# ssm_k by channels and turned on TensorE in an AdaLN / long-convolution / token-mixer kernel

## The chip, the cores and the metric

The kernel runs on one core of a Trainium2 chip. The metric is the device time of one execution in microseconds (us). Everything is float32; the large products of the mixer run as split float32 products, outside the part that is changed.

## The reference

Only what the changed part computes is kept. S is 2048 tokens, D 640 channels.

```python
mod = (silu(c) @ w_mod)                       # six rows of 640: sa, ca, ga, sb, cb, gb
h  = layernorm(q) * (1 + ca) + sa
k_shift = causal depthwise conv of k with shift_k (4 taps per channel)
kv = k_shift * v
y  = irfft(rfft(kv padded to 2S) * rfft(ssm_k padded to 2S))[:S] + kv * ssm_D
x  = q + ga * (h * y)
# then: layernorm of x, modulation with cb and sb, the token mixer (w1, gelu, w2), times gb, plus x
```

`kv * ssm_D` is done by adding `ssm_D` to element 0 of each channel's filter `ssm_k`.

## The kernel before

**Stages.** The 640 channels go in NC = 5 groups of DC = 128, `c` = 0 to 4. The long convolution of a group is a transform written as matrix products. *Step one* (`step1(side, t)`, line 222) multiplies by the constant F1, in four tiles `t` for each side: side 0 is kv, side 1 the filter; a tile is 16 matmuls into one PSUM buffer, which ScalarE copies into Z (line 232). *f2* (`f2(g)`, line 236), eight tiles a group, is the second step of both sides at once: 32 matmuls (line 246), a ScalarE copy (line 250), two VectorE products (`mul`) and two POOL combinations (`add`) into Y. *i2* and *i1* (lines 267 and 285) go back: i2 writes T2, which is the second half of the tile T_z; i1 needs the constant V1, and its PSUM result is gated: VectorE multiplies it into A1 (`gate`, line 311), POOL adds A1 to the rows of q. A1 is prepared as (q normalised) times G1 plus G0: ScalarE writes the 16 normalised row tiles (`ac`, line 301), VectorE multiplies and adds (`po`). After the last group the mixer follows, some 390 us that the change does not touch.

**Orders.** The schedule is written out by hand: each engine runs its instructions in the order of the text. In the loop over `c`, the f2 of group `c` is followed by step one of side 0 of the next group, i2, i1 with the gates, and step one of side 1 of the next group; then f2 of the next group. Three PSUM buffers go round (`psum()`, `ring`); a fourth, `tap`, holds the taps and sums of kv and also the products of w_mod. Loads go out on SP's queue, at the start some on ScalarE's.

**The first group.** kv of a group is made in four parts `g` (`kv_ops`): part 2 on POOL, 0, 1 and 3 on VectorE, eight operations of 128x512 each, into the tile X (`T_x` are other tiles, for the rows of q). The taps lie in TR, a part of the tile T_rows; `load_taps` loads them and `all_taps` copies them. At the start the parts of kv of group 0 are made while SP loads group 1 (`kv_loads`), then step one of side 0 runs on TensorE, then kv of group 1, then step one of side 1.

**The filter.** `load_ks` (line 162) brings ssm_k of a group by time, in pieces of 32 numbers, two loads of 512 KB into KSR (the first half of T_aux), and ssm_D as a row; `perm_add` (line 170) adds ssm_D, on POOL or VectorE; `perm` (line 175) is one ScalarE copy of 128x2048 into KSP (the tile P), the operand of step one's side 1. P also holds f2's products later. The ssm_k of group 1 can be loaded only after w_mod's pieces 2 and 3 have been read, since they lie in T_aux.

**The modulation.** `load_q` (line 512) loads the 32 half tiles of q and pieces 0 to 3 of w_mod; piece 4 follows after f2. `mod_part` (line 350) is a product of one piece (line 354, six matmuls), `mod_sum` a ScalarE copy of the sum, `mod_row(i)` (line 361) spreads a row over the partitions into G0, G1. VectorE's statistics of q (lines 561, 562) follow f2 of group 0, then `rstd` (line 334) takes the root on ScalarE and Newton steps on VectorE. In the tail of group 0 the order is: step one of side 0, a transposition (line 572) of the biases and of `c` with silu, i2(0), products 0 to 3, rstd, four rows of `ac`, i2(1), product 4, mod_sum, `ac`, kv part 2 on POOL, mod rows, taps, `perm_add(1)`, `perm(1)`, `ac`, `po`, i1 with the gates, step one of side 1.

## Time and profile before

| | |
|---|---|
| runs | 703.35 us median of 3 (703.0 to 708.99) |
| profiled execution | 706.67 us, its span 704.6 us |
| mean granted TensorE clock in it | 0.976 |
| busy | PE 641.4, PEld 620.4, DVE 501.5, ACT 307.8, POOL 156.1 us |
| DMA | 89.36 MB, mean 127 GB/s over the span |
| first step one starts / first f2 starts | 23.22 / 40.87 us |
| f2 of group 1 starts | 110.63 us |

PE is TensorE's matmuls, PEld its weight loads, DVE VectorE, ACT ScalarE, POOL GpSimd, SP the engine that issues most DMAs. Times within the execution count from the start of its span. The profile names a group of instructions by line, engine, operation and tile (out<-in); line 60 is the helper that records every VectorE and POOL tensor operation, so such rows are told apart by their tiles. A matmul of the program stands twice in the profile's counts where both operands are plain float32.

### The profile page before, as it was taken

The page shows a single profiled execution, that of the slowest core. Times are in us where ns is not written, and L with a number is a line of the kernel's source. Part 1 is how long each engine was busy: PE and PEld are TensorE (multiplying, and loading weights), DVE is VectorE, ACT ScalarE, POOL GpSimd, SP SyncE. Part 2 cuts the span into 40 slices and gives each one's busy share as a digit, 9 for nine tenths or more (in the row PEclk, how much of TensorE's full clock was granted, in tenths as well). Part 3 has the DMA queues.
Part 4 walks back from the last instruction along what each step waited for, and adds up shares of the span by engine and source line. Part 5 has one row for each costly group of instructions (what it writes and reads, how often), then busy time and mean ns, then how long its engine had stood idle before and what let it go on. Part 6 is the DMA issues. An engine that isn't in the chain of part 4 may idle for free.

```text
span 704.6 us, 20705 instructions
## 1 busy us (share of the span) xinstructions
PE 641.4 (91%) x9078; PEld 620.4 (88%) x9078; DVE 501.5 (71%) x846; ACT 307.8 (44%) x463; POOL 156.1 (22%) x135
## 2 busy tenths in 40 slices
PE   0699769999999999978888999999999999999997
PEld 0699569989989989758878999999999999999997
DVE  7688578969878638679886430564377699888886
ACT  0664644635745545345766420431243332333331
POOL 5297058625527328100010000000000000000000
PEclk9999979999999899799999999999999999999999
DMA  9978978346433522334030833357385634555511
GB/s 182 213 217 263 325 159 176 86 78 143 78 68 92 151 56 70 114 83 98 1 60 22 158 62 59 78 130 160 112 234 152 205 116 128 153 170 171 155 52 39
DMA packets 170848, 89.36 MB, mean 127 GB/s; under 512 B 89571, under 2 KB 160518, under 8 KB 170758
## 3 DMA queue, kind: packets, MB, share of 16 engines
q1 hardware_dynamic: 166210, 86.73, 48.8%
q10 hardware_dynamic: 4548, 1.31, 1.1%
q8 instruction: 71, 1.16, 0.7%
q14 instruction: 19, 0.16, 0.1%
HBM read 74.25 MB, written 13.76 MB: 125 GB/s over the span
## 4 chain that ended last, share of the span: by engine, by line
PE 67%; DVE 14%; DMA 6%; POOL 5%; ACT 4%; issue 3%; SPq 0%; ACTq 0%; DVEq 0%; POOLq 0%
PE pst L1059 20%; PE pst L446 17%; PE pst L246 8%; PE pst L230 7%; PE pst L275 6%; POOL y L60 4%; PE pst L1123 4%; PE pst L947 3%; DMA aux<-in_A_ssm_k_dram 3%; PE pst L294 2%; DVE aux L60 2%; DVE tap L60 1%; DVE p L60 1%; PE tap L354 1%; DVE kt L60 1%
## 5 line engine op out<-in xcount | busy, mean ns | idle before, releaser
L246 PEld LDWEIGHTS pst<-z,w 128*64 128x64 f32 x2560 | 94.7, 141 | 7.7 <-ACT z L232 7.3
L246 PE MATMUL pst<-z,w 128*64 128x64 f32 x2560 | 95.7, 240 | 6.2 <-ACT z L232 6.1
L60 POOL TENSOR_TENSOR y<-p 128x256 f32<-128x256 f32 x72 | 92.5, 1353 | 24.3 <-DVE p L60 23.9
L60 DVE TENSOR_TENSOR p<-pst,kt 128x512 f32<-128x512 f32 x80 | 52.6, 693 | 22.1 <-ACT kt L250 15.9
L230 PE MATMUL pst<-v,x 128*64 128x128 f32 x640 | 45.8, 304 | 23.2 <-POOL t L471 23.2
L232 ACT ACTIVATE z<-pst 128x1024 f32<-128x1024 f32 x40 | 45.8, 1144 | 43.9 <-PE pst L230 25.9
L230 PEld LDWEIGHTS pst<-v,x 128*64 128x64 f32 x640 | 43.8, 221 | 23.7 <-issue 23.2
L1059 PE MATMUL pst<-r_z,m_w 128*128 128x320 f32 x259 | 48.5, 309 | 1.3 <-DVE m_w L60 1.3
L275 PEld LDWEIGHTS pst<-v,y 32*128 32x128 f32 x1280 | 43.3, 210 | 6.5 <-POOL y L60 2.7
L275 PE MATMUL pst<-v,y 32*128 32x64 f32 x1280 | 45.3, 297 | 2.8 <-DVE y L60 2.1
L1047 ACT ACTIVATE m_w<-m_v 128x896 fp32r<-128x896 f32 x30 | 27.8, 948 | 42.6 <-DVE m_v L60 27.4
L230 PE MATMUL pst<-v,p 128*64 128x128 f32 x640 | 40.0, 284 | 7.0 <-DVE aux L60 4.9
L250 ACT ACTIVATE kt<-pst 128x512 f32<-128x512 f32 x40 | 25.2, 631 | 48.0 <-PE pst L246 25.6
L230 PEld LDWEIGHTS pst<-v,p 128*64 128x64 f32 x640 | 37.4, 143 | 8.3 <-DVE aux L60 5.1
L1059 PEld LDWEIGHTS pst<-r_z,m_w 128*128 128x128 f32 x259 | 40.6, 188 | 1.5 <-DVE m_w L60 1.5
L60 DVE TENSOR_TENSOR m_w<-m_v,m_w 128x896 fp32r<-128x896 f32 x30 | 32.5, 1087 | 11.2 <-ACT m_w L1047 11.2
L853 ACT ACTIVATE pst<-pst,sm 128x640 f32<-128x640 f32 x14 | 10.7, 767 | 59.3 <-PE pst L446 59.3
L60 DVE TENSOR_TENSOR tap<-tap,kt 128x512 f32<-128x512 f32 x51 | 35.6, 698 | 1.3
L60 DVE TENSOR_TENSOR kt<-in,tap 128x512 f32<-128x512 f32 x51 | 35.1, 688 | 1.5
L1059 PE MATMUL pst<-h_x,m_w 128*128 128x320 f32 x168 | 33.7, 309 | 0.0
L283 ACT ACTIVATE z<-pst 128x512 f32<-128x512 f32 x38 | 21.4, 665 | 27.9 <-PE pst L275 27.9
L1047 ACT ACTIVATE m_w<-m_p 128x896 fp32r<-128x896 f32 x13 | 12.4, 954 | 44.5 <-DVE m_p L60 27.6
(310 smaller groups left out, 1395.6 us busy)
## 6 DMA issues: line engine op xcount, KB each, us to landing
x<-in_B_w_dram SPq DMA_DIRECT2D x20, 512.0 KB
m_v<-in_B_w_dram SPq DMA_DIRECT2D x19, 384.0 KB
aux<-in_A_ssm_k_dram SPq DMA_DIRECT2D x10, 512.0 KB
m_x<-xs SPq DMA_DIRECT2D x32, 160.0 KB
out_dram<-m_x SPq DMA_DIRECT2D x32, 160.0 KB
in<-in_A_k_dram SPq DMA_DIRECT2D x36, 128.0 KB
in<-in_A_v_dram SPq DMA_DIRECT2D x36, 128.0 KB
x<-in_B_w_dram SPq DMA_DIRECT2D x10, 384.0 KB
```

Source lines behind the costliest of these rows:

```text
L60: TT = lambda eng, o, a, b, op: eng.tensor_tensor(o, a, b, op=op)
L230: pe.matmul(ps[64 * ri:64 * ri + 64, o:o + 128], lhs, F1[:, 128 * ri:128 * ri + 128], start=True, stop=True)
L232: evac = lambda: act.activation(Z[:, side, t].rearrange("p a k e -> p e a k"), ps.rearrange("p (e a k) -> p e a k", a=8, e=2), AF.Copy)
L246: pe.matmul(ps[64 * h:64 * h + 64, o:o + 64], W2[k1 // 32][:, 2 * (k1 % 32) + ri], rhs, start=True, stop=True)
L250: act.activation(kt.rearrange("p (m i) -> p m i", i=32), pv[:, :, 1], AF.Copy)
L275: pe.matmul(pp[qd // 2][:, o:o + 64], Y[p, ri, i:i + 2].rearrange("p i k -> p (i k)"), V2[p, 64 * ri:64 * ri + 64], start=ri == 0, stop=ri ...
L283: act.activation(o, i, AF.Copy)
L446: pe.matmul(ps[0:m, h, 0:320], w_.bitcast(F32R), r_[:, 320 * h:320 * h + 320].bitcast(F32R), start=first and i == 0, stop=last and i == 2)
L947: pe.matmul(ps[n][:, h, 0:320], sets[n][:, j].bitcast(F32R), r[:, 320 * h:320 * h + 320].bitcast(F32R), start=j == 0 and r is hh, stop=j = ...
L1047: act.activation(W[n][0].bitcast(F32R), A[p, w_], AF.Copy)
L1059: pe.matmul(bank[n], w[:, i].bitcast(F32R), r.bitcast(F32R), start=i == 0 and k == 0, stop=i == 6 and k == 2)
L1123: pe.matmul(acc[s][:, h, 0:320], w[:, f_].bitcast(F32R), u[r + h].bitcast(F32R), start=f_ == 0 and k == 0, stop=f_ == NF - 1 and k == 2)
```

## The change

- ssm_k of groups 0 and 1 is loaded by channels (`load_kc`, one load of 1 MB, 8 KB a channel) into KSR, and `turn` brings it into KSP: 64 small matmuls against an identity (EYE, loaded into a part of T_rows) into two PSUM buffers, and four ScalarE copies. ssm_D is loaded as columns (`dcol`) and added by one ScalarE (group 0) or POOL (group 1) instruction of 128x1. Groups 2 to 4 keep `load_ks`, `perm_add` and `perm`.
- The first ssm_k is issued behind the first part of v, ahead of the rest of v; the order of v stays 0, 2, 1, 3. The first w2 constant goes out behind the first v load of group 1.
- kv of group 0 goes into T_y (`x0`), and X is left to group 1; kv of group 1 is now written ahead of step one in the text.
- Step one of group 0: tiles 0 and 1 of side 1, then the four of side 0, then tiles 2 and 3 of side 1.
- q and w_mod: q 0 to 3, piece 0, q 4 to 7, piece 1 and the taps before f2; q 8 to 15, piece 3 and ssm_k of group 1 in f2's fourth tile; pieces 2 and 4, now in the second half of T_z, after f2. The transposition and silu move into f2's sixth tile.
- In the tail of group 0: the five products right after step one (order 0, 1, 3, 2, 4), the loads of k and v of group 2, mod_sum, i2(0), mod rows 0 and 1, rstd, mod row 2, eight rows of `ac`, i2(1), eight rows, all of `po`, then kv part 2 on POOL, `turn`, the taps, the next `load_ks`.

The order on each engine follows the text of both kernels.

```diff
@@ -40,9 +40,8 @@
     v2 = np.tile(np.concatenate([c, -s, s, c], 1), (4, 1))
     ang = 2 * np.pi * ((1 + 4 * k1)[:, None, None] * (32 * n1[None, None, :] + n2[None, :, None]) % 8192) / 8192
     v1 = np.tile(np.stack([np.cos(ang), np.sin(ang)], 1).reshape(64, 4096) / 2048, (2, 1))
-    sel = np.zeros((128, 128))
-    sel[0, 0:64] = sel[1, 64:128] = 1
-    small = np.concatenate([f1.reshape(128, 256), v2, np.eye(128)[:, 0:36], np.tile(np.eye(2), (64, 1)), sel], 1)
+    small = np.concatenate([f1.reshape(128, 256), v2, np.eye(128)[:, 0:36], np.tile(np.eye(2), (64, 1)),
+                            np.eye(128)], 1)
     return {"small": small.astype(np.float32), "w2": w2.reshape(128, 4096).astype(np.float32),
             "v1": v1.astype(np.float32)}
 
@@ -111,7 +110,7 @@
     V1 = T_v1[:, 0:4096].rearrange("p (r n m) -> p r n m", r=2, n=32)
     SM = T_v1[:, 4096:4518]
     F1, V2, ID, MK = SM[:, 0:256], SM[:, 256:384], SM[:, 384:420], SM[:, 420:422]
-    TR, DR = T_rows[:, 0:256], T_rows[:, 512:576]
+    TR, EYE, DR = T_rows[:, 0:256], T_rows[:, 256:384], T_rows[:, 512:576]
 
     PS_, PT, PW = T_t[:, 0:512], T_t[:, 512:1024], T_t[:, 1024:1280].rearrange("p (s i) -> p s i", s=4)
     CB, SB, GB = T_kt[:, 0:640], T_kt[:, 640:1280], T_rows[:, 0:640]
@@ -131,6 +130,7 @@
     msk = small(1)
     su, sq, msb = small(16), small(16), small(1)
     epsc = small(1)
+    dcol = small(2)
     B1C, B2C = cols[:, 0:14], cols[:, 14:30]
 
     tap = psp.tile([128, 1024], F32, name="tap", tag="pst3", bufs=1)
@@ -177,11 +177,27 @@
                        KSR.rearrange("p (e i n) -> p i e n", e=2, i=32), AF.Copy)
 
 
+    def load_kc(c):
+        sync.dma_start(KSR, dram(ssm_k, DC * c * S, [[S, 128], [1, S]]), max_dma_last_dim=4096)
+
+    def turn():
+
+        for s in range(2):
+            ps = psum()
+            for n in range(16):
+                for h in range(2):
+                    pe.matmul(ps[64 * h:64 * h + 64, 64 * n:64 * n + 64],
+                              KSR.rearrange("p (a n) -> p n a", n=32)[:, 16 * s + n], EYE[:, 64 * h:64 * h + 64],
+                              start=True, stop=True)
+            for o in (0, 8):
+                act.activation(KSP.rearrange("p i (n e) -> p n e i", e=2)[:, 16 * s + o:16 * s + o + 8],
+                               ps.rearrange("p (n e i) -> p n e i", n=16, e=2)[:, o:o + 8], AF.Copy)
+
     def taps():
 
         act.activation(TAP, TR.rearrange("p (i s) -> p s i", s=4), AF.Copy)
 
-    def kv_ops(g, eng=dve):
+    def kv_ops(g, eng=dve, x=X):
         S_, T_, W_ = (SV, TV, TAP) if eng is dve else (PS_.rearrange("p (n i) -> p n i", i=64),
                                                        PT.rearrange("p (n i) -> p n i", i=64), PW)
         w = lambda s: W_[:, None, s, :].to_broadcast([128, 8, 64])
@@ -190,7 +206,7 @@
         for s in (2, 1, 0):
             ops.append(lambda s=s: TT(eng, T_, kx(s), w(s), ALU.mult))
             ops.append(lambda: TT(eng, S_, S_, T_, ALU.add))
-        ops.append(lambda: TT(eng, X.rearrange("p (n i) -> p n i", i=64)[:, 8 * g:8 * g + 8], S_,
+        ops.append(lambda: TT(eng, x.rearrange("p (n i) -> p n i", i=64)[:, 8 * g:8 * g + 8], S_,
                               VX[:, 8 * g:8 * g + 8], ALU.mult))
         return ops
 
@@ -219,12 +235,12 @@
         return ops
 
 
-    def step1(side, t, later=False):
+    def step1(side, t, later=False, x=X):
 
         ps = psum()
         for a in range(8):
             i = 8 * t + a
-            lhs = KSP[:, i] if side else X.rearrange("p (m i) -> p i m", i=32)[:, i]
+            lhs = KSP[:, i] if side else x.rearrange("p (m i) -> p i m", i=32)[:, i]
             o = 512 * (a % 2) + 128 * (a // 2)
             for ri in range(2):
                 pe.matmul(ps[64 * ri:64 * ri + 64, o:o + 128], lhs, F1[:, 128 * ri:128 * ri + 128], start=True,
@@ -461,10 +477,14 @@
     load_halo(0)
     for g in range(4):
         load_k(0, g, both)
-    for g in (0, 2, 1, 3):
+    load_v(0, 0, both)
+    act.dma_start(EYE, dram(c_small, 422, [[550, 128], [1, 128]]))
+    load_kc(0)
+    for i in range(2):
+        act.dma_start(dcol[:, i:i + 1], dram(ssm_D, DC * i, [[1, 128], [1, 1]]))
+    for g in (2, 1, 3):
         load_v(0, g, both)
     sync.dma_start(SM, dram(c_small, 0, [[550, 128], [1, 422]]))
-    load_ks(0, act)
 
     def all_taps():
         for eng, t in ((pool, PW), (dve, TAP)):
@@ -477,14 +497,17 @@
 
     all_taps()
     load_taps(1, act)
-    run(kv_ops(2, pool))
+    x0 = T_y[:, 0:2048]
+    act.activation(KSR[:, 0:1], KSR[:, 0:1], AF.Identity, bias=dcol[:, 0:1])
+    turn()
+    run(kv_ops(2, pool, x0))
+    run(kv_ops(0, dve, x0))
+    kv_loads(1, 0)
     load_w2c(0)
-    run(kv_ops(0))
-    kv_loads(1, 0)
-    run(kv_ops(1))
+    run(kv_ops(1, dve, x0))
     kv_loads(1, 1)
     kv_loads(1, 2)
-    run(kv_ops(3))
+    run(kv_ops(3, dve, x0))
     kv_loads(1, 3)
     load_w2c(1)
     for h in range(2):
@@ -492,29 +515,32 @@
         sync.dma_start(stg[7 * h + 6:7 * h + 7, :], dram(b1, 864 * h + 736, [[128, 1], [1, 128]]))
     sync.dma_start(stg[14:30, :], dram(b2, 0, [[128, 16], [1, 128]]))
     sync.dma_start(stg[30:35, :], dram(c, 0, [[128, 5], [1, 128]]))
-    perm_add(0)
-    perm(0)
     all_taps()
-    load_taps(2)
-    for t in range(4):
-        step1(0, t)
-        lay_w2(0, t)
     run(kv_ops(2, pool))
     run(kv_ops(0))
     run(kv_ops(1))
-    for t in range(4):
-        step1(1, t)
-
-
     three = lambda t: [t[:, 640 * j:640 * j + 640] for j in range(3)]
-    pl = [three(t) for t in (T_v1, T_v1[:, 1920:3840], T_aux, T_aux[:, 2048:3968], P)]
-
-    def load_q():
-        for j in range(16):
+    pieces = T_v1, T_v1[:, 1920:3840], T_z[:, 4096:6016], T_aux[:, 2048:3968], T_z[:, 6144:8064]
+    pl = [three(t) for t in pieces]
+
+    def load_q(j0, j1, *kk):
+        for j in range(j0, j1):
             for b in range(2):
                 sync.dma_start(XH[j // 8][64 * b:64 * b + 64, j % 8], dram(q, (16 * b + j) * D, [[32 * D, 64], [1, D]]))
-        for kk in range(4):
-            mod_load(0, kk, (T_v1[:, 0:1920], T_v1[:, 1920:3840], T_aux[:, 0:1920], T_aux[:, 2048:3968])[kk])
+        for k_ in kk:
+            mod_load(0, k_, pieces[k_][:, 0:1920])
+
+    load_q(0, 4, 0)
+    load_q(4, 8, 1)
+    load_taps(2)
+    step1(1, 0)
+    step1(1, 1)
+    for t in range(4):
+        lay_w2(0, t)
+        step1(0, t, x=x0)
+    step1(1, 2)
+    step1(1, 3)
+
 
     fill = kv_ops(3)
 
@@ -547,7 +573,13 @@
             if c == 0 and g < 4:
                 lay_w2(1, g)
                 if g == 3:
-                    load_q()
+                    load_q(8, 16, 3)
+                    load_kc(1)
+            if c == 0 and g == 5:
+                ps = psum()
+                pe.transpose(ps[:, 0:36], stg, ID[0:36, 0:36])
+                act.activation(cols, ps[:, 0:36], AF.Copy)
+                act.activation(sil, cols[:, 30:35], AF.Silu)
             dv(-(-len(fill) // max(6 - g, 1)))
             if c and cn is not None and g == 3:
                 perm_add(cn)
@@ -565,24 +597,15 @@
             if c + 3 < NC:
                 load_taps(c + 3)
         if c == 0:
-            mod_load(0, 4, P[:, 0:1920])
+            mod_load(0, 2, pieces[2])
+            mod_load(0, 4, pieces[4])
+            TT(pool, KSR[:, 0:1], KSR[:, 0:1], dcol[:, 1:2], ALU.add)
             for t in range(4):
                 step1(0, t)
-            ps = psum()
-            pe.transpose(ps[:, 0:36], stg, ID[0:36, 0:36])
-            act.activation(cols, ps[:, 0:36], AF.Copy)
-            act.activation(sil, cols[:, 30:35], AF.Silu)
-            i2(0)
-            for kk in range(4):
+            for kk in (0, 1, 3, 2, 4):
                 mod_part(tap, kk, pl[kk])
                 if kk == 1:
                     sync.dma_start(T_v1[:, 0:4096], c_v1, max_dma_last_dim=4096)
-                if kk == 2:
-                    load_ks(1)
-            rstd(rs1, nm1, 0, 16)
-            run(ac[0:4])
-            i2(1)
-            mod_part(tap, 4, pl[4])
             load_k(2, 1)
             load_k(2, 2)
             load_v(2, 2)
@@ -593,18 +616,21 @@
             load_k(2, 3)
             load_v(2, 3)
             mod_sum(tap, T_kt[:, 0:640])
-            run(ac[4:8])
+            i2(0)
+            mod_row(0, T_kt[:, 0:640])
+            mod_row(1, T_kt[:, 0:640])
+            rstd(rs1, nm1, 0, 16)
+            mod_row(2, T_kt[:, 0:640])
+            run(ac[0:8])
+            i2(1)
+            run(ac[8:16])
+            run(po)
             pool.tensor_scalar(PW, TR.rearrange("p (i s) -> p s i", s=4), 1.0, None, op0=ALU.mult)
             run(kv_ops(2, pool))
-            for i in range(3):
-                mod_row(i, T_kt[:, 0:640])
+            turn()
             taps()
             load_taps(3)
-            perm_add(1, dve)
-            perm(1)
             load_ks(2)
-            run(ac[8:16])
-            run(po[0:2])
             fill.extend(kv(3, ((0,), (1, 2), (3,))))
         elif cn is not None:
             for t in range(2):
@@ -658,8 +684,6 @@
                 dv(3)
             elif c:
                 k0 = step1(1, 0, True)
-            elif half:
-                run(po[2:4])
             gate(c, ps, half)
         spill(c)
         if c:
```

## Prediction

> **What bounds the kernel now.** I read the page first (engine shares), then the chain of waits in order of time, then the timeline and the windows of its first 111 us, because the diff touches nothing behind that point. In the chain each row is start, duration, what the end waited for.
>
> ```profile
> PE 641.4 (91%) x9078; PEld 620.4 (88%) x9078; DVE 501.5 (71%) x846; ACT 307.8 (44%) x463; POOL 156.1 (22%) x135
> ...
> 14.67 4.77 DMA aux<-in_A_ssm_k_dram
> 23.22 16.48 PE pst L230 x256
> ...
> 77.19 14.79 DMA aux<-in_A_ssm_k_dram
> ...
> 99.98 2.18 DVE aux L60
> ...
> 103.53 5.93 PE pst L230 x64
> ...
> 110.63 14.37 PE pst L246 x377
> ```
>
> TensorE is busy 91% of the span, so a gain must come from a stretch where it isn't. There are two. It does nothing until 23.22 us, and between 77 and 110.63 the chain leaves it: a 14.79 us wait for ssm_k, then a VectorE multiply, then step one at a poor rate. The second stretch, closer (timeline rows: start, duration, engine, line; window rows: PE, PEld, DVE, ACT, POOL busy with counts, then granted clock, DMA share, GB/s):
>
> ```profile
> 76.50 10.57 SPq L164 DMA_DIRECT2D aux<-in_A_ssm_k_dram  x2
> 92.43 2.13 ACT L176 ACTIVATE p<-aux 128x2048 f32<-128x2048 f32 x1 [3.75 <-DMA in<-in_A_k_dram]
> 97.65 4.50 DVE L60 TENSOR_TENSOR aux<-aux,g 128x1024 f32<-128x1024 f32 x2 [1.46 <-ACT aux L301]
> 102.25 1.23 DVE L60 TENSOR_TENSOR aux<-pst,aux 128x1024 f32<-128x1024 f32 x1
> ...
> 100.00:102.00 2.00, 0.00 (x0) 0.00 (x0) 2.00 (x1) 0.00 (x0) 1.92 (x2) 0.81 0.84 190
> 104.00:106.00 2.00, 2.00 (x24) 2.00 (x22) 1.90 (x4) 0.00 (x0) 1.89 (x2) 0.50 0.77 176
> ```
>
> The second ssm_k is issued at 76.50 (SP is held 10.57 us by it), ScalarE can permute it only at 92.43, VectorE's gate products end at 102.15 with one gate behind them, and TensorE, which needs the PSUM buffer that the gates read, stands still and then runs step one's 64 records in 5.93 us at a granted clock of 0.50. Line 230 on the same operand takes 7.18 us for 128 at the full clock (row below), so 3.59 for 64: 2.3 us go to the clock.
> The Trainium skill (TensorE: Matmul & The Clock Gate, Part 1) says the array drops to half rate after an idle window of about 3.4 us and needs as long a busy window to return; the trace agrees with the drop: 0.50 follows a window without a matmul.
>
> **Part 1, the start up to f2(0).** Removed: two ssm_k loads in 128-byte pieces, POOL's additions of ssm_D, the permutation on ScalarE. Added: one load by channels (kc, 1.05 MB), an identity, two columns of ssm_D, one small ScalarE addition, `turn` (64 matmuls of 64x64, which the profile counts twice, so 128 records), four ScalarE copies. Step one of the filter side now brackets that of the kv side.
>
> ```profile
> 0.00:2.00 2.00, 0.00 (x0) 0.00 (x0) 0.74 (x7) 0.00 (x0) 0.19 (x4) 1.00 0.04 8
> 2.00:4.00 2.00, 0.00 (x0) 0.00 (x0) 0.00 (x0) 0.00 (x0) 0.00 (x0) 1.00 0.76 170
> 4.00:6.00 2.00, 0.00 (x0) 0.00 (x0) 0.92 (x2) 0.00 (x0) 1.10 (x1) 1.00 1.22 232
> 24.00:26.00 2.00, 2.00 (x22) 2.00 (x20) 0.00 (x0) 1.02 (x1) 0.00 (x0) 1.00 1.27 212
> 26.00:28.00 2.00, 2.00 (x36) 2.00 (x34) 0.00 (x0) 1.35 (x2) 0.00 (x0) 1.00 1.12 183
> ...
> 4.84 4.55 SPq L150 DMA_DIRECT2D in<-in_A_v_dram  x4
> 13.32 1.14 ACTq L160 DMA_DIRECT2D rows<-in_A_shift_k_dram  x2
> 21.62 1.28 ACT L176 ACT_TABLE_LOAD   x1 [21.62 <-DMA aux<-in_A_ssm_k_dram]
> 22.43 0.69 DVE L60 TENSOR_TENSOR x<-tap,in 128x512 f32<-128x512 f32 x1
> 26.65 1.16 ACT L232 ACTIVATE z<-pst 128x1024 f32<-128x1024 f32 x1 [1.63 <-PE pst L230]
> 32.51 7.18 PE L230 MATMUL pst<-v,p 128*64 128x128 f32 x128
> 40.87 18.98 PE L246 MATMUL pst<-z,w 128*64 128x64 f32 x511 [1.19 <-ACT z L232]
> 59.74 8.24 PE L230 MATMUL pst<-v,x 128*64 128x128 f32 x127
> ```
>
> *kc lands.* SP issues its four v loads from 4.84 in 4.55 us, 1.14 each; kc takes the second place, 6.0. Issued by then are taps 0.13, halo 0.09, k 1.05 and the first v 0.26 MB, 1.53 MB; the first three windows moved (8+170+232) GB/s x 2 us = 0.82 MB. The other 0.71 at about 220 GB/s ends at 9.2. kc itself goes at 205 GB/s if its rows do no better than those of k and v (5.1 us), at 392 if like w_mod's (2.7, row below); I take 300 for it shares the engines with v: 3.5 us, 12.7, and 1.3 (estimate) to its release: 14.0. It can be 12; and 17.5 if it takes the 6.95 us between the chain's 14.67 and the release at 21.62 that ssm_k has now.
> The Trainium skill (Trainium Kernel Development and Optimization, Key Constraints) says that loads of SP's and ScalarE's queues run on the same 16 engines and interleave, which speaks against the early load; by it alone kc would wait for all of v too, another 0.8 MB or some 4 us, and part 1 would end 4 us later, inside the upper bound below.
>
> *turn.* ScalarE issues two tap loads behind kc (1.14, their release held by kc), loads its table (1.28), adds ssm_D (0.3): 16.7. Line 246 has turn's shape, 64 columns of weights, 64 moving: 18.98/512 = 37 ns. Turn's weights are strided as X's are; line 230 with X takes 8.24/127 = 65 ns, with P's unbroken rows 7.18/128 = 56, so 9 more: 46. The first TensorE work is slow now (22 records in window 24 to 26, 36 in the next, 1.64 times): 40 records at 75 ns, 88 at 46, 7.0 us. Bounds: 4.7 (37 ns, no slow start) and 10.0 (65 ns, and slow). So 23.7; the second half's two copies at 0.56 (2.23/4 for 128x512, row below): 24.8.
> By the skill's clock page (Part 1) the first 3.4 us run at half rate: 37 records at 92, 91 at 46, 7.6 us, and 0.6 later.
>
> *Step one.* Four tiles at 7.18 in all and four at 8.24: 40.2; the last copy 1.16: f2(0) starts at 41.4 against 40.87. TensorE used to wait for VectorE's last kv product (22.43 + 0.69); by 28.4, when it gets there now, x0 is long there. The earlier start thus buys the price of turn, no more: **+0.5 us**, bounds 37.1 (kc at 12, turn 4.7) and 47.9 (17.5 and 10.0). The tap loads behind kc are needed at 23.1 and land some 3 us after 15.1; identity, ssm_D columns and the place T_y for x0 cost nothing on the path, covered by kc's wait.
>
> **Part 2, f2(0) to the end of w_mod's products.** f2 18.98 us, 0.8 more (estimate) for the transposition of 0.25 put between its tiles, which takes one of three PSUM buffers: 61.2. Step one 8.24: 69.4. Then five w_mod products, now all ahead of i2.
>
> ```profile
> 33.81 0.63 SPq L104 DMA_DIRECT2D xb<-in_const_w_dram  x1
> 40.10 11.46 SPq L515 DMA_DIRECT2D xa<-in_A_q_dram  x16
> 72.89 2.35 PE L354 MATMUL tap<-v,sm 128*32 128x320 f32 x24
> ...
> 74.00:76.00 2.00, 2.00 (x24) 0.76 (x21) 1.93 (x7) 1.98 (x3) 0.00 (x0) 1.00 1.04 392
> ```
>
> A product is 2.35/2 = 1.18, five are 5.9: 75.3, if the data are there. SP's queue: with kc in place of ssm_k (2.7 for 5.1 us) the loads of c=1 end 2.4 us earlier, so the second w2 goes at 31.4, not 33.81. Now q follows it after 6.3 us, with two tap loads between; without these I take 4.1 (estimate): q from 35.5, not 40.10. A q load takes 11.46/16 = 0.72 of SP; 32 of them, two w_mod pieces and the taps: 60.8. Behind them come w_mod 3, kc(1), and pieces 2 and 4, which need T_z's second half and so the end of f2 (61.2): 4.0 MB at 392 GB/s, 10.2 us, with the release at 72.5. The last product wants it at 74.1. Covered by 1.6 us only.
> SP then stands at the v1 constant until product 1 has been read (71.8); behind it wait the k and v loads of c=2. v1 2.1 MB and the first three pairs of k and v are in by 82, POOL wants them at 86, i1 wants v1 at 93.
>
> **Part 3, from there to f2(1).** The order of ScalarE decides.
>
> ```profile
> 62.06 0.88 DVE L561 BATCH_NORM_STATS2 sm<-xa 128x6 f32<-128x320 f32 x2
> 69.17 3.79 PE L275 MATMUL pst<-v,y 32*128 32x64 f32 x124 [0.64 <-ACT z L232]
> 72.81 2.23 ACT L283 ACTIVATE z<-pst 128x512 f32<-128x512 f32 x4 [2.10 <-PE pst L275]
> 77.98 0.21 DVE L562 BATCH_NORM_AGGREGATE sm<-sm 128x2 f32<-128x12 f32 x1
> 78.23 0.31 ACT L338 ACTIVATE sm<-sm 128x16 f32<-128x16 f32 x1 [1.88 <-DVE sm L562]
> 80.16 1.65 ACT L301 ACTIVATE aux<-xa,sm 128x128 f32<-128x128 f32 x4 [1.62 <-DVE sm L343]
> 84.69 0.72 ACT L358 ACTIVATE kt<-tap 96x640 f32<-96x640 f32 x1
> 86.83 0.70 ACT L372 ACTIVATE g<-pst 128x640 f32<-128x640 f32 x1
> 87.57 1.55 DVE L60 TENSOR_TENSOR g<-pst,g 128x640 f32<-128x640 f32 x2 [7.50 <-ACT g L372]
> 87.59 5.75 PE L294 MATMUL pst<-z,v 64*64 64x64 f32 x256 [0.76 <-ACT g L372]
> ```
>
> i2(0) 3.79: 79.1 (mod_sum's 0.72 beside it); its copies 2.23: 81.3; two mod rows 1.4: 82.7; table and root 1.6: 84.3. The statistics, 16.1 us from 62.06 to 78.19 now and starting 2.2 us after f2, are done at 79.5, ahead of that. VectorE's Newton steps 1.6: 85.9. Eight normalised rows (1.65 for four) 3.3: 89.2; i2(1)'s copies 91.4; eight rows 94.7; turn's copies 96.9. TensorE meanwhile: turn from 87.5, when the g products (1.55) free its buffer, 6.0 at the warm rate: 93.5; the two i1 5.75 in all: 99.3; step one 7.18: 106.5; last copy 1.1: f2(1) at **107.6** against 110.63. VectorE's four products at the slow 2.25 each end at 99.2 and the two gates (1.23 each) by 101.7; the PSUM buffers they free are wanted at 101.1 and 102.9. Moving the gate products ahead of POOL's work costs nothing while this cover of 0.7 to 1.2 us holds, and us for us beyond it. After f2(1) every stage has the same instructions, with ssm_k of c=2 issued some 6 us earlier against its use: nothing.
>
> Sum: -3.0 us. The profiled execution took 706.67 (span 704.6 and 2.1 around it) and would take 703.7; it lies 3.3 above the median of the runs, 703.35, so my forecast for the median is **700.3**.
>
> **The rivals.** *Early* (0.28): kc at 12, turn at line 246's 37 ns without a slow start, q from 33 and so the last w_mod at 70. Then f2(0) starts at 37.1 (-4.3), and i1 runs warm, 4.5 for 5.75: -8.5, 694.8. For it: three prices taken from their lower rows, all seen. Against: the first records were slow in this profile, and w_mod's cover of 1.6 us eats 2.7 of the 4.3 unless q moves too.
> *Turn late* (0.13), the other side: kc behind k and v lands at 17.5, as when a channel load does no better than the scattered one (the change then doesn't do what it says), turn 10.0. f2(0) at 47.9, +6.5 on my sum: 3.5 slower, 706.8. It decides once f2(0) starts after 43.9. For it: the DMA share is above 1.2 in window 4 to 6; against: 392 GB/s where rows are long.
> *Loads late* (0.12): the last 4.0 MB at q's 229 GB/s (0.164 MB per 0.72 us) instead of 392: 17.5 us, release 80, products end at 81.2: +5.9, 2.9 slower, 706.2. i2(0) is queued behind the products, so all of it shows. Against: the window at 74 to 76.
>
> **How the numbers follow.** My sum has 0.47, with its own range 697.4 to 703.4 (i1 warm, 0.5 to 3 us of part 1 either way). The range 694.0 to 707.5 takes in the rivals' prices and leaves about 0.1 on either side. One per cent, 7.0 us, is about what a measurement of this kernel tells from no change: below 696.3 lie nine tenths of *early* and 0.07 of my own case, 0.32; above 710.4 four tenths of the two late ones, which can come together, and 0.02 besides, 0.12; 0.56 between.
>
> **What would show it.** Right: the first line of `turn` near 16.7 and 7 us long, f2(0) within 39.5 to 43.5, no wait of 14 us for ssm_k, w_mod products in one stretch ending near 75, no clock of 0.50 in step one of c=1, f2(1) near 107.6, every later stage as long as before. Wrong: TensorE idle at the w_mod products for a DMA (loads), the start beyond 44 (turn), or a loss behind f2(1), for which I have no mechanism.

## The result and the profile after

| | before | changed |
|---|---|---|
| median of the runs measured together | 701.57 us | 711.2 us |
| time, changed / before | | 1.0125, 95% interval 1.0095 to 1.0156 |
| profiled execution (span) | 706.67 us (704.6) | 708.09 us (706.3) |
| first step one / f2 of group 0 starts | 23.22 / 40.87 us | 27.01 / 45.06 us |
| w_mod's products end | 83.8 us | 82.2 us |
| f2 of group 1 starts | 110.63 us | 118.70 us |

The change costs 1.25%, 8.8 us, where 3 us less were forecast. The two profiled executions differ by 1.4 us only, because that of before lies 5.1 us above its median and that of the changed kernel 3.1 below its own. In before's, TensorE ran at half clock in the tail of a later group: the same 128 records of i2 took 4.92 and 7.11 us there (3.80 at full clock), in a stretch at a mean granted clock of 0.77 (1.00 in the changed kernel). First the timeline of before (start, duration, engine, line), then its window (length, PE busy, granted clock, DMA share, GB/s).

```profile
285.88 4.92 PE L275 MATMUL pst<-v,y 32*128 32x64 f32 x128 [0.51 <-DVE y L60]
293.02 7.11 PE L275 MATMUL pst<-v,y 32*128 32x64 f32 x128
```

```profile
280.00:310.00 30.00, 27.26 (x636) 0.77 0.22 69
```

f2 of group 1 is therefore the better mark: it starts 8.07 us later, near the 8.8 us of the ratio. The chain of waits of the changed kernel, in order of time (start, duration, what):

```profile
6.41 7.39 DMA aux<-in_A_ssm_k_dram
...
16.93 8.11 PE pst L189 x128
25.07 1.90 ACT p L193 x2
...
27.01 16.91 PE pst L246 x236
...
45.06 13.05 PE pst L262 x325
58.10 0.64 issue
...
89.52 6.71 PE pst L291 x124
96.23 8.21 PE pst L189 x115
...
118.70 2.62 PE pst L262 x62
```

The 14.79 us wait for ssm_k is gone, as meant. In its place stand two passes of `turn` (line 189), 8.11 and 8.21 us, and i2(1) at 6.71 us. The timeline (start, duration, engine, line; in brackets the idle time before it and what ended it) shows the rest:

```profile
27.01 5.38 PE L246 MATMUL pst<-v,p 128*64 128x128 f32 x64 [1.98 <-ACT p L193]
32.22 8.17 PE L246 MATMUL pst<-v,y 128*64 128x128 f32 x128
...
34.06 7.52 SPq L529 DMA_DIRECT2D xa<-in_A_q_dram  x8
52.83 13.58 SPq L529 DMA_DIRECT2D xb<-in_A_q_dram  x16
67.68 1.56 SPq L363 DMA_DIRECT2D z<-in_w_mod_dram  x2
...
78.48 1.28 PE L370 MATMUL tap<-z,sm 128*32 128x320 f32 x12 [1.70 <-DMA z<-in_w_mod_dram]
80.97 1.28 PE L370 MATMUL tap<-z,sm 128*32 128x320 f32 x12 [1.21 <-DMA z<-in_w_mod_dram]
89.36 6.87 PE L291 MATMUL pst<-v,y 32*128 32x64 f32 x124
96.16 8.28 PE L189 MATMUL pst<-rows,aux 128*64 128x64 f32 x128
101.04 2.09 ACT L193 ACTIVATE p<-pst 128x512 f32<-128x512 f32 x2
...
110.77 6.71 PE L246 MATMUL pst<-v,p 128*64 128x128 f32 x118 [1.09 <-issue]
```

Step one waits 1.98 us for turn's copies, and its first 64 records take 5.38 us where the next 128 take 8.17. The last two pieces of w_mod leave SP only at 67.68 (the last q went at 52.83 + 13.58 = 66.4), and TensorE waits 1.70 and 1.21 us for them. Then i2(1), turn and i1 follow each other on TensorE almost without a gap, and step one behind them stops once for 1.09 us. The windows (PE, PEld, DVE, ACT, POOL busy, granted clock, DMA share, GB/s) show at which clock, and that the DMA engines are full while the products wait:

```profile
20.00:22.00 2.00, 2.00 (x37) 2.00 (x36) 1.90 (x4) 0.82 (x1) 0.20 (x1) 1.00 0.99 358
28.00:30.00 2.00, 2.00 (x24) 2.00 (x22) 1.90 (x4) 0.37 (x1) 0.00 (x0) 0.55 0.78 176
30.00:32.00 2.00, 2.00 (x26) 2.00 (x24) 1.90 (x4) 0.73 (x1) 0.69 (x1) 0.60 0.90 203
...
76.00:78.00 2.00, 0.78 (x9) 0.12 (x3) 1.93 (x7) 0.00 (x0) 0.19 (x1) 1.00 1.04 398
...
92.00:94.00 2.00, 2.00 (x44) 2.00 (x43) 1.86 (x5) 1.50 (x4) 1.92 (x3) 0.50 0.65 144
98.00:100.00 2.00, 2.00 (x36) 2.00 (x34) 1.71 (x1) 2.00 (x7) 1.92 (x2) 0.53 0.02 4
100.00:102.00 2.00, 2.00 (x38) 2.00 (x36) 0.82 (x1) 2.00 (x5) 1.92 (x2) 1.00 0.00 0
```

Before, TensorE stood for much of the time between the products and the last of step one, behind the filter's load and the gates; now it is busy there, with turn, which was not there before, and with both i2, which used to stand ahead of the last products.

### The profile page after: what moved, and what is told of

It reads as the page before. It is cut to its first block, busy times and chain, and to the rows that moved or that the text cites. A ratio compares the mean times of both kernels' runs of the same rounds, so it can differ in the third digit from the quotient of the medians.

```text
span 706.3 us, 21226 instructions
## 1 busy us (share of the span) xinstructions
PE 655.6 (93%) x9334; PEld 635.6 (90%) x9334; DVE 502.2 (71%) x844; ACT 312.4 (44%) x470; POOL 156.4 (22%) x134
## 4 chain that ended last, share of the span: by engine, by line
PE 68%; DVE 13%; POOL 6%; DMA 5%; ACT 4%; issue 3%; SPq 1%; ACTq 0%; DVEq 0%; POOLq 0%
PE pst L1083 20%; PE pst L462 17%; PE pst L246 7%; PE pst L262 6%; PE pst L291 6%; POOL y L59 5%; PE pst L1147 3%; PE pst L971 3%; PE pst L310 3%; PE pst L189 2%; DMA aux<-in_A_ssm_k_dram 2%; DVE tap L59 1%; DVE kt L59 1%; DMA in<-in_A_k_dram 1%; SPq L144 1%
## 5 line engine op out<-in xcount | busy, mean ns | idle before, releaser
L262 PE MATMUL pst<-z,w 128*64 128x64 f32 x2560 | 96.2, 240 | 6.9 <-ACT z L248 6.1
L59 DVE TENSOR_TENSOR m_w<-m_v,m_w 128x896 fp32r<-128x896 f32 x30 | 32.5, 1087 | 11.1 <-ACT m_w L1071 11.1
L246 PE MATMUL pst<-v,x 128*64 128x128 f32 x512 | 36.4, 300 | 0.0
L246 PEld LDWEIGHTS pst<-v,x 128*64 128x64 f32 x512 | 34.5, 221 | 0.6
L189 PE MATMUL pst<-rows,aux 128*64 128x64 f32 x256 | 16.4, 309 | 16.9 <-DMA rows<-in_A_shift_k_dram 16.9
```

The source lines that it names most:

```text
L59: TT = lambda eng, o, a, b, op: eng.tensor_tensor(o, a, b, op=op)
L189: pe.matmul(ps[64 * h:64 * h + 64, 64 * n:64 * n + 64], KSR.rearrange("p (a n) -> p n a", n=32)[:, 16 * s + n], EYE[:, 64 * h:64 * h + 64] ...
L246: pe.matmul(ps[64 * ri:64 * ri + 64, o:o + 128], lhs, F1[:, 128 * ri:128 * ri + 128], start=True, stop=True)
L262: pe.matmul(ps[64 * h:64 * h + 64, o:o + 64], W2[k1 // 32][:, 2 * (k1 % 32) + ri], rhs, start=True, stop=True)
```

## The experiments

Theories at the outset: the loads (the order on SP makes w_mod's last pieces late, and i2 is queued behind the products); the turn (its own time on TensorE, twice); and the clock (TensorE at half rate in step one and i2(1)).

**The start.** Filter of group 0 loaded by time again, step one side 0 first; kv of group 0 stays in T_y, and everything from f2(0) on is as changed.

```diff
-    load_kc(0); turn()            # with the loads of v and the order of step one
+    load_ks(0, act); perm_add(0); perm(0)
```

> The changed kernel with the start put back for group 0: ssm_k by time, perm_add and perm, loads of v and w2 and the order of step one as before; kv still goes to T_y, the rest as changed. Theory 'turn': TensorE's pass over the filter at the start (16.92 to 25.03, then 1.97 us of copies) is what makes f2 of group 0 start at 45.06 for 40.87, so f2(0) comes back to 41 to 42 and the time falls by 3 to 4 us. Rival 'loads': the tail of group 0 is set by w_mod's last piece (landed at 80.9), so an earlier f2(0) only makes TensorE wait longer there: f2(0) falls by 4 but f2(1) by less than 1.5, and the time with it.

Measured: 711.16 us, ratio 1.0126 (1.0097 to 1.0154), against 1.0125 with the whole change. f2(0) started at 41.9, 3.2 us earlier, and f2(1) at 124.5, 5.8 later: the last q left SP at 72.4 instead of 66.4 and the last pieces behind it at 73.6 instead of 67.7, so this run moves the loads too. With the second filter loaded by time as well, only the orders of the change are left:

```diff
-    load_kc(0); turn()   ...   load_kc(1); turn()
+    load_ks(0, act); perm_add(0); perm(0)   ...   load_ks(1); perm_add(1); perm(1)
```

> Both filters by time, start as before, and only the changed orders left: loads of q and w_mod, their places, the products ahead of i2, the gate work. Theory 'turn': 8 to 11 us below the changed kernel, that is level with the kernel before or up to 3 us faster, as its second wait for ssm_k is gone. Rival 'orders': 3 us or more slower than the kernel before still.

Measured: 705.85 us, ratio 1.0061 (1.0022 to 1.0101); f2(1) started at 116.3. Its timeline, at the products:

```profile
77.28 2.35 PE L370 MATMUL tap<-aux,sm 128*32 128x320 f32 x12 [5.81 <-DMA aux<-in_w_mod_dram]
82.78 1.28 PE L370 MATMUL tap<-z,sm 128*32 128x320 f32 x12 [1.27 <-DMA z<-in_w_mod_dram]
```

Whatever the start wins, the products lose to the loads: they reach piece 3 some 6 us before it is there. So undoing the start alone brings nothing. The products end at 84.0, no earlier than before (83.8), and f2(1) follows 32.3 us behind them instead of 26.8, as both i2 now stand behind the products: that is what the orders cost.

**The tail: the turn or the loads.** First the second filter by time, behind pieces 2 and 4; the start as changed.

```diff
-    load_kc(1)                      # in f2's fourth tile
+    load_ks(1)                      # behind mod_load(0, 4)
-    turn()
+    perm_add(1); perm(1)
```

> The changed kernel with the second filter loaded by time again (two scattered loads behind w_mod's pieces 2 and 4), perm_add on POOL behind the root, perm in turn's place; the start as changed. Theory 'turn': the second pass of turn (8.28 us of TensorE between i2(1) and i1) and its copies (4 x 1.04 us) lie on the path: f2 of group 1 comes 5 to 8 us earlier than 118.7. Rival 'orders': ScalarE's and VectorE's order (rows, products, gates) ends the tail, so f2(1) moves by less than 2 us, or gets later since the scattered load holds SP for 10 us ahead of v1 and of k and v of group 2.

Measured: 704.82 us, ratio 1.0037 (1.0008 to 1.0066): some 6 of the 8.8 us come back. Its timeline:

```profile
78.01 2.33 PE L370 MATMUL tap<-z,sm 128*32 128x320 f32 x24
...
97.36 6.83 PE L310 MATMUL pst<-z,v 64*64 64x64 f32 x256 [1.86 <-ACT z L299]
```

The products run without a wait (74.8 to 80.3, though f2(0) ended 1.4 us later), and from their end to f2(1) at 112.6 lie 32.3 us instead of 36.5. A turn of 8.3 us thus costs 4.2 net: without it TensorE stands 1.86 us for ScalarE and runs i1 cold, 6.83 us instead of 4.5. The other runs agree: the stretch takes 36.5 to 37.4 us in the four traces with turn unaltered and no fillers, and 32.3 to 33.6 in the three that have the change's tail with the filter by time. Then the loads by themselves: pieces 2 and 4 are not loaded, and their products read piece 3.

```diff
-            mod_load(0, 2, pieces[2])
-            mod_load(0, 4, pieces[4])
```

> The changed kernel without the loads of w_mod's pieces 2 and 4; their products read piece 3 (a part of the modulation is thus computed from the wrong rows). Theory 'loads': TensorE's waits of 1.70 and 1.21 us at those products go, all behind them moves up, the time falls by 2.5 to 3 us or more (v1 and the k and v of group 2 land earlier too). Theory 'turn': the products end 2.9 us earlier but part of it is eaten by ScalarE's chain: 1 to 3 us; the main loss stays.

Measured: 706.8 us, ratio 1.0063 (1.0035 to 1.0091). Products 74.8 to 80.4, turn 8.1 us, f2(1) at 117.4: by the ratios two pieces less give back some 4 us of the loss, though f2(1) is only 1.3 us earlier in the trace; the tail stays long. And only the place of the 1 MB on SP:

```diff
-                    load_kc(1)      # in f2's fourth tile
+            load_kc(1)              # behind mod_load(0, 4)
```

> Changed kernel, only the load by channels of group 1's filter stands behind w_mod's pieces 2 and 4 on SP instead of ahead of them; turn stays. It divides what the second filter by time (704.82 us, f2(1) at 112.6) gave back between the order of the loads and the turn in the tail. If the loads carry it: the 2.9 us wait at the products goes, products end near 80, f2(1) near 116, some 708 us. If the tail's turn carries it: 36.4 us still lie between the products' end and f2(1), against 32.3 with the filter by time, so even without a wait 4 us stay lost. If the wait is set by the bytes of q and not by this 1 MB: no change, products end 82, f2(1) 118 to 119.

Measured: 708.98 us, ratio 1.0083 (1.0046 to 1.0121). The interval overlaps that of the whole change, so 3 us is the likeliest gain and none cannot be excluded. In its profiled execution (714.66 us) the products waited three times, 1.14 to 1.21 us, and ended at 85.2, f2(1) at 121.7, and the last q left SP at 71.8: that trace does not show the earlier products that the load theory asked for.

**The turn's price.** Small matmuls on an idle PSUM tile keep TensorE busy at the start and through the tail.

```diff
+    warm(20)        # ahead of the first step one
...
+    warm(16)        # after the first mod row;  warm(12) after the third
```

> The changed kernel with matmuls of 64x64 on the identity into unused columns of tap: 20 between turn and step one at the start, 16 ahead of the second mod row and 12 ahead of i2(1); they only keep TensorE busy. Theory 'clock': the granted clock of 0.50 from 90 to 99 (and 0.55 to 0.60 from 28 to 32) comes from TensorE's pauses before it; with them filled i2(1) takes 3.8 for 6.87 us, turn 6 to 7 for 8.28 us, the first two tiles of step one 3.6 for 5.38 us, and the time falls by 3 to 5 us. Rival: turn is bound by its weight loads and the tail by ScalarE, so i2(1) gets short, but turn stays near 7 to 8 us and the time falls by less than 2 us.

Measured: 720.32 us, ratio 1.0261 (1.0213 to 1.0309). The start failed as an experiment: the filler writes the tile `tap`, in which VectorE makes the sums of kv, so TensorE stood for 13.06 us until 38.3 and began step one at 42.4. The tail can still be read, by its timeline and one window:

```profile
102.40 3.80 PE L295 MATMUL pst<-v,y 32*128 32x64 f32 x128
106.54 8.26 PE L189 MATMUL pst<-rows,aux 128*64 128x64 f32 x128 [0.33 <-DVE g L59]
```

```profile
110.00:112.00 2.00, 2.00 (x36) 2.00 (x35) 2.00 (x1) 2.00 (x7) 1.92 (x2) 1.00 0.00 0
```

At clock 1.00 i2(1) takes 3.80 instead of 6.87 us, but turn takes 8.26 as before, and the tail, products' end to f2(1), 35.5 instead of 36.5 us. The clock is worth 1 us net here, and that is a lower bound: the fillers themselves hold i2(1) back, which starts 9.7 us behind the products' end instead of 7.2. Next, turn with weights from neighbouring columns:

```diff
-    KSR.rearrange("p (a n) -> p n a", n=32)[:, 16 * s + n]
+    KSR.rearrange("p (n a) -> p n a", n=32)[:, 16 * s + n]
```

> The changed kernel with turn's weights taken from 64 neighbouring columns instead of every 32nd (the filter comes out in a wrong order, the work is the same). Theory 'stride': 54 ns a record in the full clock windows of turn come from the strided weight load, so turn's records fall to about 37 ns as line 262's, turn to 5 us. Rival 'shape': 54 ns are the price of these matmuls however the weights lie; turn stays at 7 to 8 us.

The timeline of this kernel:

```profile
17.71 6.51 PE L189 MATMUL pst<-rows,aux 128*64 128x64 f32 x128 [17.71 <-DMA in<-in_A_v_dram]
101.59 5.63 PE L189 MATMUL pst<-rows,aux 128*64 128x64 f32 x128
```

Measured once: 710.31 us. In the timeline turn takes 6.51 and 5.63 us: the stride of 32 costs 1.6 and 2.6 us a pass. The stretch from the products' end to f2(1) is 34.4 instead of 36.5 us, so most of what turn lost there was gained; the time hardly moves, for the products ended only at 87.1 in this run. Last, the copies out of PSUM, walked with 16 neighbouring outputs innermost:

```diff
-    ps.rearrange("p (n e i) -> p n e i", n=16, e=2)[:, o:o + 8]
+    ps.rearrange("p (n e i) -> p i n e", n=16, e=2)[:, :, o:o + 8]
```

> The changed kernel with turn's four copies walked the other way: the 16 neighbouring numbers of KSP innermost, PSUM read in steps. Theory: the 1.04 us of a copy of 128x512, twice that of i2's, come from writing with a stride of 256 bytes; then they fall to 0.55 to 0.65 and f2(0) comes 0.8 us earlier. Rival: a strided side costs the same wherever it is: 1.0 us stays.

Measured once: 709.47 us. ScalarE's timeline has two copies in 1.09 us, as my sum had them, against 1.90 to 2.19 in the changed kernel; f2(0) started at 44.7, 0.4 us earlier though turn had begun 0.4 later, the 0.8 us expected.

```profile
25.46 1.09 ACT L193 ACTIVATE p<-pst 128x512 f32<-128x512 f32 x2 [2.77 <-PE pst L189]
```

The products ended at 85.8 and f2(1) started at 123.2 here, at 87.1 and 121.4 in the run before, with loads in the order of the change: the profiled execution of the change itself, with 82.2 and 118.70, is a favourable one.

**The wait of before, taken away in another manner.** If ssm_k of group 1 no longer has to wait for w_mod's pieces, the load by time can go early without any turn. A first form put pieces 2 and 3 into the tile of k and v.

```diff
-    pl = ... (T_v1, T_v1[:, 1920:3840], T_aux, T_aux[:, 2048:3968], P)
+    pl = ... (T_v1, T_v1[:, 1920:3840], T_in[:, 192:2112], T_in[:, 2112:4032], P)
+            load_ks(1)              # behind mod_load(0, 4)
```

> The kernel before with one thing moved: w_mod's pieces 2 and 3 go into the k and v tile of group 1, free after its kv, and the second ssm_k, still by time, is issued behind piece 4, ahead of the v1 constant. If the loss before lies in the late ssm_k alone, perm comes 4 us earlier (88 for 92.4) and step one of the second group no longer stands behind the gate: 3 to 5 us faster than before. Rival: the scattered load then delays v1 (needed at 87.6) and k and v of group 2 by what it saves: within 1 us of before.

Measured: 725.61 us, ratio 1.0334 (1.0285 to 1.0384). The chain of waits names the reason:

```profile
65.46 13.26 DMA in<-in_w_mod_dram
```

The loads stood in the text ahead of VectorE's last operations on kv of group 1, so these waited for the loads (and read w_mod where k and v had been), and f2(0) stopped from 56.0 to 80.9. A misplaced edit, no answer on the idea. The mended form: piece 2 where piece 3 lay, piece 3 into the tile of k and v behind f2, then piece 4 and the filter.

```diff
-    pl = ... (T_v1, T_v1[:, 1920:3840], T_aux, T_aux[:, 2048:3968], P)
+    pl = ... (T_v1, T_v1[:, 1920:3840], T_aux[:, 2048:3968], T_in[:, 192:2112], P)
+            mod_load(0, 3, T_in[:, 192:2112])
             mod_load(0, 4, P[:, 0:1920])
+            load_ks(1)
```

> Kernel before, with one thing altered: w_mod's piece 2 goes where piece 3 lay, piece 3 into the tile of k and v once group 1's kv is made, so that the filter of group 1 (by time, two loads) can be issued behind piece 4, near 68 us, and not at 76.5 behind product 2. If the 14.8 us wait for ssm_k sets the tail of the kernel before: the permutation starts near 85 instead of 92.4, f2(1) starts at 105 to 108 against 110.6, 3 to 5 us faster. If the loads take their turn anyway (all bytes of q, w_mod, ssm_k, k and v of group 2 go at some 225 GB/s): products or kv part 2 get later by what ssm_k gets earlier, and f2(1) stays within 1.5 us of 110.6.

Measured: 700.0 us, ratio 0.9975 (0.9949 to 1.0002), f2(1) at 109.9. The timeline tells why a wait of 14.8 us brought so little:

```profile
84.37 0.39 SPq L581 DMA_DIRECT2D v<-in_const_v_dram  x1
92.61 4.11 PE L294 MATMUL pst<-z,v 64*64 64x64 f32 x142 [5.10 <-DMA v<-in_const_v_dram]
```

V1, which i1 needs, stands on SP behind ssm_k's issues and is now the one that comes last (5.10 us). So V1 on ScalarE's queue:

```diff
-                    sync.dma_start(T_v1[:, 0:4096], c_v1, max_dma_last_dim=4096)
+                    act.dma_start(T_v1[:, 0:4096], c_v1, max_dma_last_dim=4096)
```

> The kernel before with group 1's filter issued behind w_mod's piece 4 (700.0 us), and the constant V1 now issued on ScalarE's queue at the same place of the text. In the run without this, i1 waited 5.1 us for V1 (92.6), because V1 stood on SP behind 17 us of ssm_k's issues; ssm_k itself was there at 89.7. If the place on SP makes V1 late: V1 is issued near 77 instead of 84, i1 starts at 89 to 90.5, f2(1) at 106.5 to 108, 697 to 699 us. If the bytes make it late (ssm_k, V1 and the first k and v of group 2 share the engines): V1 lands a little earlier and ssm_k later, i1 or step one's side 1 waits as long as before, f2(1) at 109 to 111, 699.5 to 701.5 us.

Measured: 700.79 us, ratio 0.9969 (0.9938 to 0.9999). Its timeline:

```profile
67.90 16.39 SPq L164 DMA_DIRECT2D aux<-in_A_ssm_k_dram  x2
...
79.37 0.41 ACTq L581 DMA_DIRECT2D v<-in_const_v_dram  x1
93.27 5.67 PE L294 MATMUL pst<-z,v 64*64 64x64 f32 x256 [3.59 <-DMA v<-in_const_v_dram]
105.90 3.71 PE L230 MATMUL pst<-v,p 128*64 128x128 f32 x64 [1.10 <-DVE aux L60]
```

V1 goes at 79.37 and still lands only at 93.3; ssm_k holds SP for 16.39 instead of 13.93 us, and f2(1) starts at 110.8. So the place on SP was not what made V1 late; the second theory, the bytes, fits. This and the version before it are the best found, 0.3% under before by the comparison, and only here does the interval just leave 1 out; against the same mark the changed kernel stands at 1.0125.

**The order of the loads.** Only the orders are left of the change, and SP's queue is put in another order: piece 3 ahead of q 8 to 12, pieces 2 and 4 next, then the last q and ssm_k.

```diff
-                    load_q(8, 16, 3)
+                    mod_load(0, 3, pieces[3][:, 0:1920])
+                    load_q(8, 13)
...
             mod_load(0, 4, pieces[4])
+            load_q(13, 16)
+            load_ks(1)
```

> Both filters by time and the start as before, so that only the orders of the change are left, with SP's queue put in another order: w_mod's piece 3 ahead of q 8 to 12, then pieces 2 and 4, q 13 to 15 and the filter of group 1. With the old order (705.85 us) the products waited 5.8 us for piece 3 and 1.3 us for piece 2. If it is the bytes ahead of the pieces that made them late: products from 69 to 75 without a wait, f2(1) near 75 + 32.3 = 107.3, 697 to 701 us. If the statistics of q or ssm_k are late instead (q 13 to 15 land after 70): i2(1) and i1 move back by the same, f2(1) at 111 to 114, 701 to 705 us.

Measured: 702.97 us, ratio 1.0003 (0.9972 to 1.0034). f2(0) took 23.8 us in its trace (42.2 to 66.0), products 74.2 to 81.3 with one wait of 1.41, f2(1) at 114.9. The orders of the change can be had at no cost this way, not at a gain. And the reverse, before with pieces 0 and 1 between the first q:

```diff
+    load_q(0, 4, 0)
+    load_q(4, 8, 1)
...
-                    load_q()
+                    load_q(8, 16, 2, 3)
```

> The kernel before with one part of the change alone: q 0 to 3, w_mod's piece 0, q 4 to 7 and piece 1 in this order (they used to go q 0 to 15, piece 0, piece 1). If the bytes of the two pieces hold q back at some 225 GB/s: the last q is issued 7 to 9 us later (70 to 72 instead of 63.5), pieces 2 to 4 behind it by as much less the two pieces, so within 1 us of where they were, and products are not later than 79 (piece 3); statistics of q wait for xb, rstd and the rows of q normalised move back 2 to 4 us, f2(1) at 111 to 114, 702 to 705 us. If a DMA share near 1.0 during f2 of group 0 is what makes TensorE stand without a visible releaser there: f2(0) takes 20 to 23 us with pauses put down to issue, as in the runs that load the pieces early, against 19.0 without any. If neither: f2(0) 19.0, f2(1) at 110.6, 701.6 us.

Measured: 703.99 us, ratio 1.0007 (0.9971 to 1.0044), f2(1) at 110.5. The timeline, then the windows of this kernel (columns of the windows as above):

```profile
54.05 13.40 SPq L515 DMA_DIRECT2D xb<-in_A_q_dram  x16
...
61.31 1.44 PE L246 MATMUL pst<-z,w 128*64 128x64 f32 x35 [1.71 <-issue]
```

```profile
54.00:58.00 4.00, 4.00 (x117) 4.00 (x115) 3.14 (x6) 1.29 (x2) 4.00 (x4) 1.00 0.93 305
58.00:62.00 4.00, 2.29 (x63) 2.15 (x60) 1.69 (x3) 0.63 (x1) 4.00 (x5) 1.00 1.06 256
```

The last q leaves SP at 67.45 against 63.49 before: two pieces ahead push it back by 4.0 us, not by the 7 to 9 expected. The products (75.8 to 85.2) do not wait, since i2(0), which in the kernel before runs ahead of them, covers it. f2(0) takes 20.9 us, with a pause of 1.71 that nothing visible ends.

## Why the prediction was wrong

f2(1) was forecast at 107.6 and came at 118.70, 11.1 us later. By the prediction's own steps:

| term | forecast | measured | off by |
|---|---|---|---|
| TensorE starts turn | 16.7 | 16.92 | +0.2 |
| turn, group 0 | 7.0 | 8.11 | +1.1 |
| its last two copies | 1.1 | 1.98 | +0.9 |
| step one, eight tiles | 15.4 | 16.9 | +1.5 |
| f2(0) and step one after it | 28.0 | 28.3 | +0.3 |
| five products | 5.9 | 8.8 | +2.9 |
| products' end to turn(1) | 12.2 | 14.0 | +1.8 |
| turn, group 1 | 6.0 | 8.28 | +2.3 |
| i1 | 5.75 | 4.5 | -1.3 |
| step one of the filter and its copy | 8.3 | 9.8 | +1.5 |

Two steps failed. The products were to end at 75.3 and ended at 82.2, 6.9 us late: 4.0 from the start, where turn, its copies and step one were dearer, and 2.9 from the waits for w_mod. With a start as forecast the loads would have held them all the same, as the last piece was there only at 80.9. And the stretch from there to f2(1) was to take 32.3 us and took 36.5. Against before, the forecast let the products end 8.5 us earlier; they ended 1.6 earlier.

*Right.* The load by channels: there at 6.41 + 7.39 = 13.8 (forecast 14.0), and turn's start. i2(0), the five products' own time (5.5 in the runs without a wait), and that nothing behind f2(1) moves: 589.4 us follow it in the profiled execution, 588.4 in the mended form of before with its early ssm_k. The wait for ssm_k went, as the change says. f2(0) with step one is right by luck: the 0.8 us that I allowed for the transposition between its tiles was taken by a pause of TensorE of 0.64 (last section).

*Wrong: the price of turn.* I took 46 ns a record from f2's row plus a surcharge for stride, 7.0 and 6.0 us. It is 63 to 65, the upper of my two bounds, and with neighbouring columns 44 to 51. The row that was really nearest, step one with X's strided columns at 65 ns, I had used only as a bound. The copies, taken from i2's copies of the same size, cost 0.95 to 1.10 each instead of 0.56; the walk of the outputs makes the difference. Together 4.3 us of the terms above.

*Wrong: step one at full clock.* The slow first records, which I put into turn, came in step one: windows 28 to 32 at 0.55 and 0.60.

*Wrong: w_mod's cover of 1.6 us.* I let q end at 60.8, counting the two pieces between its loads by the 0.6 us of their issue. q ended at 66.4. With pieces ahead on the kernel before, q was 4.0 us later; part of the rest comes from q's first loads, which now leave at 34.06 behind the loads of group 1 (7.52 us for 8, against 5.32 for 8 in that kernel). The last 4.0 MB then took from 66.46 to 80.9, 277 GB/s, between the 392 that I used and the 229 of the rival. The rate of the engines was not the error: they moved 398 to 415 GB/s in every window from 70 to 82. But the four loads did not have it to themselves: 5.3 MB moved between 66.4 and 81, with the last of q and the first of V1, issued at 75.75, among them. The rival loads late had the products' end at 81.2; they ended at 82.2. I gave it 0.12; it came near, but the slow rate that it rests on is in none of these windows.

*Wrong: the turn on the path.* I wrote that ScalarE decides the tail, but my sum ran along TensorE, turn, i1 and step one in a row, and there TensorE did decide. Its terms were off. Turn was 2.3 us too cheap. It was to start when the g products free its buffer; in fact i2(1) held it, which waited for the mod rows, started at 89.36 and ran at half clock to 96.2 (+1.8). Step one behind i1 was 1.5 longer, 1.09 of it another pause of TensorE. i1 ran at full clock (-1.3). With the filter by time the stretch takes 32.3 us without any turn, as long as my sum had allowed it with turn: the net price of this turn, 4.2 us, is the miss of the tail.

The rival turn late put the deciding point at f2(0) after 43.9; f2(0) started at 45.06, by turn's price alone, for the load came in time. Both late rivals, given 0.12 and 0.13 as alternatives, came true in part and together. I had noted that as possible and gave 0.12 to a time above 710.4, but ended the range at 707.5 with 0.1 above it, and their prices simply added (5.9 and 6.5 us on 700.3) lie beyond it.

What the runs show as the cause. In the traces f2(1) is 8.07 us later than before because the products end only 1.6 us earlier and the stretch behind them is 9.7 us longer: 5.5 with the new order, which puts both i2 behind the products (32.3 us for 26.8 with both filters by time), and 4.2 with turn. The order pays only if the products come as much earlier, and the loads of q and w_mod do not let them. By the ratios, 6 of the 8.8 us (3 to 9 by the intervals) come back with the second filter by time, which takes out its turn and takes its 1 MB from ahead of the pieces; the orders alone cost 4.3 (1.5 to 7), so the two are not a clean sum; with the orders alone, another order of the same loads brings the time level with before. How the loads' share divides between kc's place and the pieces themselves is not settled: the intervals of those runs overlap. The profiled execution of before, my base, was itself some 5 us long in a group that the change does not touch; I corrected 3.3 of it.

## What to carry to other kernels

Before replacing a wait, find the next thing that would be waited for: here the data of the stretch (q, w_mod, ssm_k, V1, k and v) already filled the engines (a share of 0.96 to 1.11 from 64 to 84 in the kernel before), so an early load moved the wait to a neighbour: to w_mod's pieces in the changed kernel, to V1 in the two with the filter by time early (5.10 and 3.59 us). A layout change moved from DMA to TensorE is free only while TensorE stands anyway; price it by the row with the same stride, and count it on the path once the wait that covered it is gone. A load put between others costs those behind it more than its issue (two pieces 4.0 us where their issues take 1.2).

## What the runs showed of the hardware

- Turn's records cost the same at both clocks: 36 in 2 us at a granted clock of 0.53 and 38 at 1.00 (98 to 102), and a pass takes 8.26 us in the run with fillers, all at 1.00, against 8.28. i2 (6.87 us for 3.80) and i1 (6.83 for 4.5) do slow down. What bounds turn is thus not the rate of the array; its weights' stride is part of it (6.51 and 5.63 us against 8.11 and 8.28).
- TensorE lost its clock after a stop of 1.98 us, behind 8.1 us of turn: step one's records took 55 ns up to 28, and then its first two tiles ran at 0.55 to 0.60. With the other walk of the copies the stop was 1.19 us and the first 64 records took the same 5.38. The Trainium skill (TensorE: Matmul & The Clock Gate, Part 1) has the rate fall after an idle window of about 3.4 us. This trace differs, unless turn's small matmuls count for little as activity, which no run here separates.
- A ScalarE copy of 128x512 out of PSUM takes 0.55 us when 16 neighbouring outputs are written in a row and 0.95 to 1.10 when the walk jumps to another part of the row at each output.
- TensorE paused in f2(0), released by nothing visible, in all ten traces whose pieces of w_mod go early and whose q still runs during f2 (0.2 to 3.3 us in all, DMA share up to 1.08), and in none of the three that load q alone there (19.0 us, share 0.77 to 0.82 from 46 to 58). The run with fillers, whose f2(0) came after most loads (mean share 0.51), had none either. The traces say what it waits for. Every such pause, those in i1 and step one of the tail too, begins at the same place in TensorE's recorded instructions (matmuls and weight loads above all), 193 above a multiple of 256, in the middle of a tile, where nothing new has to be waited for; it ends 1.3 to 1.7 us after a packet of 16 KB has landed on the DMA queue of kind instruction (in the changed kernel one landed at 57.29 and TensorE went on at 58.74, one at 109.29 and TensorE went on at 110.77). The pages of before and of the changed kernel have one such packet for each 256 of these instructions (2 x 9078 and 2 x 9334; packets, MB, share):

```profile
q8 instruction: 71, 1.16, 0.7%
```

```profile
PE 655.6 (93%) x9334; PEld 635.6 (90%) x9334; DVE 502.2 (71%) x844; ACT 312.4 (44%) x470; POOL 156.4 (22%) x134
...
q8 instruction: 73, 1.20, 0.7%
```

So TensorE stands there for its own next instructions, which come in by DMA like the data: 1.96 us ahead of f2(1) in the changed kernel, none in the profiled execution of before. That the loads in front make these packets late is an association, as no run took a load away for this alone.
